# Eight-pass transformer kernel: the first half chunk's maxima turned four steps earlier, and two low parts moved from VectorE to Pool

## Chip, cores and metric

One NeuronCore of a Trainium2 chip runs the kernel. The metric is the device time of one execution in microseconds (us). The time before is 1330.38 us, the median of 3 runs (1329.99 to 1331.14). The profiled execution shown below is another run of the same program.

## The reference

The input x is 2048 tokens by 512 features, in fp32. Four residual layers run one after the other, A, B, A, B, each on the layer norm of x. There are 32 heads of 16 features.

```python
def _A_ref(x, ...):   # linear attention with a learned feature map
    q, k, v = split_heads(x @ wqkv)
    phi_q = concat(softmax(q @ w_phi), softmax(-q @ w_phi))
    phi_k = concat(softmax(k @ w_phi), softmax(-k @ w_phi))
    o = phi_q @ (phi_k.T @ v) / (phi_q @ sum(phi_k) + 1e-6)
    return merge_heads(o) @ wo

def _B_ref(x, ...):   # four segments of 512 tokens, causal softmax plus a memory
    for s in range(4):
        p = softmax(qs @ ks.T * scale + mask)
        o = g * (phi(qs) @ M) / (phi(qs) @ z + 1e-6) + (1 - g) * p @ vs
        M, z = M + phi(ks).T @ vs, z + sum(phi(ks))
    return merge_heads(o) @ wo
```

Only layer B, which runs twice, is touched by the change.

## The kernel before

**Layer B's loop.** Each of the 4 segments has 4 chunks c of 8 heads, and each chunk two half chunks, so that 32 half chunks m are attended in order (m // 8 is the segment). One half chunk takes R = 5 steps of a counter k: `attend` (step m*5 on) makes the five products of keys and queries that become softmax weights. The loop starts at k = BEGIN = -25, so 25 steps run ahead of the first attended product. In them the first queries and keys are projected, while what is left of layer A's second pass (`side`) goes on being computed on the same engines. `steps` writes all of this out; what stands at which step is in tables of text. `BEFORE` is the table for negative k: "k1/2" is two steps of the projection of chunk 1's keys, "v0/2" two steps of a block of values, "max0" the step that is moved here. An entry with "<" ahead is done in front of the step's row work and side work, one without it behind them.

**Row maxima.** Softmax needs each query row's maximum. `maxima(m)` computes the products of a half chunk once more in five rounds, and VectorE (DVE) reduces each to a column of the tile `mxs` by a fused add-mask-and-max with a read of the accumulator behind it. For m = 0 and m = 1 the ten rounds run from k = MAXIMA = -17 to -8, those of m = 0 in the first five. `put_maxima(m)` then turns `mxs` into rows by four 32x32 transposes on DVE into the tile `mt`, and three steps later a DMA on SyncE's queue (SP) writes these rows into row 63 and row 127 of the query tile `e` (tag e8). `attend` multiplies 64 rows where `maxima` multiplied 63; row 63 holds the maxima, so the difference comes out of the matmul. So the first attended product of m, a TensorE (PE) matmul `lg<-e,e`, waits for the transfer `e<-mt`.

**Stacks.** A projection of queries or keys leaves PSUM as `raw` (tag tb3), and `projected` splits it in a high part (ScalarE, tile `ta`) and a low part (raw minus high, line 1075, tile `ta`). `stack(m, side)` copies these three times into the rows of the tile `e` of the chunk's set: three SP DMAs of 128 KB for the queries and three for the keys of a half chunk. `maxima(m)` and `attend(m)` read them. The stack of m = 2, the first of chunk 1, is issued at k = -4 and k = -3; its maxima start at k = 0. The two projections that it needs end at k = -17 (queries) and k = -15 (keys), and their low parts follow a step later. In `projected` all low parts are made by DVE as long as k < R, and by Pool from then on.

**Order.** Every engine's instructions stand in the order in which the program records them (`Ordered` and `held` put each behind the one before it). The fused maxima alone have a higher priority. SP works its queue in order: a DMA that waits for its data holds all behind it. Around the change the SP queue reads: store of a layer A block (`x<-xr`), maxima of m = 0 (`e<-mt`), stack of m = 2 (six times `e<-ta`), stack of m = 3 (six more), maxima of m = 1.

**Names in the trace.** All of the engines' rows but the PE's have line 155 (the helper `Ordered`), matmuls line 177 and PE transposes 181. `g`, `lg`, `mx` and `my` are PSUM tiles (`lg` attended products, `g` also projections and every other round of maxima), `P` the softmax weights or features, `KN` the summed keys of layer A.

Of the kernel before, what the change touches and what calls it, by code (L numbers as in the profile page):

```python
# [7 lines left out]
F32 = mybir.dt.float32  # L8
# [25 lines left out]
R = 5  # L34
# [10 lines left out]
MAXIMA = -17  # L45
# [49 lines left out]
7.0 <max | 7.1 fin P/4              | 7.2 P/5           | 7.3 P/4 | 7.4  # L95
"""
BEFORE = {-25: "load q0", -24: "sq0 sq1", -23: "k0", -22: "sk0 n n", -21: "sk1 v0/2 n n", -20: "v0/2 n n",
          -19: "n n", -18: "v1 n n q1/2", -17: "q1/2", -16: "k1/2", -15: "k1/2", -11: "v2", -9: "max0"}


@with_exitstack
def interleave_kernel(ctx, tc, x_in, a_wqkv, a_wphi, a_wo, b_wq, b_wk, b_wv, b_wo, b_beta,
                      c_ident, c_mask, c_bd, out):
    nc = tc.nc
    MUL, ADD, SUB, MAX, MIN = ALU.mult, ALU.add, ALU.subtract, ALU.max, ALU.min
# [14 lines left out]
    def T2(tag, bufs, dt=F32, shape=(P, 512)):  # L120
        return sp.tile(list(shape), dt, tag=tag, bufs=bufs, name=nm(tag))
# [41 lines left out]
    dve, act, pool, sync = [Ordered(e) for e in (nc.vector, nc.scalar, nc.gpsimd, nc.sync)]  # L163
# [821 lines left out]
    class LayerB:  # L985
# [80 lines left out]
        def projected(self, s, c, m, pp):  # L1066

            d = self.st[s, c]
            hi, lo = d["part", m] = [T2("ta1", TA, F32R) for _ in range(2)]
            raw = T2("tb3", TB3)  # L1070
            act.copy(raw, pp)

            def parts():
                act.copy(hi, raw)
                (pool if self.k >= R else dve).tensor_tensor(out=lo, in0=raw, in1=hi.bitcast(F32), op=SUB)
            todo = [parts]
            if not (s == 0 if m == 0 else s == NSEG - 1):
                e = d["phi", m] = T2("tb2", TB2)

                def features():  # L1080
                    act.activation(e, raw, AF.Relu, scale=-1.0)
                    act.activation(e, e, AF.Exp, scale=-1.0)

                def clipped():
                    act.activation(raw, raw, AF.Relu)

                def added():
                    if m == 0:
                        pool.tensor_scalar(raw, raw, 0.0, None, op0=MAX)
                    pool.tensor_tensor(out=e, in0=raw, in1=e, op=ADD)  # L1090
                todo += [features] + [clipped] * m + [added]
            return todo
# [511 lines left out]
```

## Time and profile before

| What | us |
|---|---|
| median of the runs | 1330.38 (1329.99 to 1331.14) |
| profiled execution, its own time | 1334.12 |
| its span, first to last instruction | 1332.4 |
| PE matmul busy | 1276.0 |
| DVE busy | 1077.4 |
| ACT busy | 834.8 |
| Pool busy | 752.4 |
| mean granted PE clock | 0.99 |

The busy sums are averages over stages with different limits, so the prediction reads one stage: the start of layer B's loop, at 250 to 305 us of the span in the first layer B and at 900 to 955 us in the second. In a row of the timeline stand start, duration, engine, line, operation, tiles and shape, and, in brackets, the time the engine stood idle before it and what ended that.

### The profile page before, as it was taken

How to read it: one execution, taken by the hardware profiler on the slowest of the kernel's cores; microseconds unless marked ns; L12 is line 12 of the kernel's file. 1: busy time of each engine (PE TensorE's matmuls, PEld its weight loads, DVE VectorE, ACT ScalarE, POOL GpSimd, SP SyncE). 2: the span in 40 equal slices, each digit the busy share in tenths (PEclk: the TensorE clock that was granted, in tenths of full speed). 3: DMA queues.
4: the chain of work that ended last, by engine and by line, in shares of the span. 5: the costliest groups of instructions: out<-in, count | busy, mean ns of one | idle time of the engine just before them, and what ended most of it. 6: DMA issues, size and time to landing. Idle time of an engine off the chain costs nothing.

```text
span 1332.4 us, 41983 instructions
## 1 busy us (share of the span) xinstructions
PE 1276.0 (96%) x16488; PEld 989.9 (74%) x16488; DVE 1077.4 (81%) x3503; ACT 834.8 (63%) x1210; POOL 752.4 (56%) x1120
## 2 busy tenths in 40 slices
PE   7999989989999999999999998899899999999987
PEld 6887868857777777777668886787677777777765
DVE  4776678768998998998857766787799999898895
ACT  5556444638778778677644433464477877877754
POOL 1568765405657767666324446562247767776653
PEclk9999999989999999999999998999899999999999
DMA  6388537625555545546451103565446545544432
GB/s 209 104 328 259 168 123 226 185 81 161 166 163 159 168 110 146 164 113 166 136 168 55 64 33 128 171 194 158 111 135 197 172 127 170 147 129 123 121 83 80
DMA packets 134420, 196.59 MB, mean 148 GB/s; under 512 B 15440, under 2 KB 61648, under 8 KB 133456
## 3 DMA queue, kind: packets, MB, share of 16 engines
q1 hardware_dynamic: 133408, 193.80, 48.3%
q8 instruction: 131, 2.15, 0.7%
q14 instruction: 65, 0.53, 0.1%
q10 hardware_dynamic: 816, 0.11, 0.1%
HBM read 101.05 MB, written 39.85 MB: 106 GB/s over the span
## 4 chain that ended last, share of the span: by engine, by line
PE 75%; DVE 16%; ACT 3%; issue 3%; DMA 2%; POOL 1%; SPq 1%; DVEq 0%; ACTq 0%; POOLq 0%
PE g L177 59%; PE lg L177 6%; PE g L181 4%; PE mx L177 3%; DVE g L155 3%; DVE U L155 2%; DVE mx L155 2%; DVE my L155 2%; PE lg L181 2%; PE my L177 1%; DVE es L155 1%; ACT P L155 1%; DVE mxs L155 1%; SPq L155 1%; DMA P<-in 1%
## 5 line engine op out<-in xcount | busy, mean ns | idle before, releaser
L155 ACT ACTIVATE P<-lg 128x1024 f32<-128x1024 f32 x316 | 324.1, 1026 | 98.3 <-PE lg L177 80.1
L155 POOL TENSOR_SCALAR_AFFINE_SELECT P<-P 128x256 f32<-128x256 f32 (+1 forms) x448 | 189.8, 441 | 241.6 <-ACT P L155 223.2
L155 DVE CUSTOM_DVE_ANT_0 mx<-mx,mask 128x512 f32<-128x512 f32 (+2 forms) x316 | 158.9, 503 | 51.2 <-PE my L177 40.7
L155 DVE CUSTOM_DVE_ANT_0 g<-g,mask 128x128 f32<-128x128 f32 (+3 forms) x392 | 189.4, 537 | 6.1 <-PE g L177 5.8
L177 PE MATMUL g<-hh,wqk 64*128 64x512 f32 (+1 forms) x960 | 181.4, 393 | 0.6 <-SPq L155 0.5
L177 PE MATMUL g<-w,oh 64*128 64x512 f32 (+2 forms) x848 | 162.3, 380 | 2.7 <-ACT oh L155 2.6
L155 DVE CUSTOM_DVE_ANT_0 my<-my,mask 128x512 f32<-128x512 f32 (+2 forms) x316 | 163.5, 517 | 0.0
L177 PE MATMUL lg<-e,e 64*128 64x512 f32 (+1 forms) x1010 | 144.8, 343 | 10.5 <-ACT P L155 7.5
L177 PE MATMUL g<-P,v 128*32 128x128 f32 (+3 forms) x2064 | 151.6, 433 | 0.2
L177 PE MATMUL g<-w,hh 64*128 64x512 f32 (+1 forms) x672 | 145.6, 399 | 2.3 <-ACT w L155 1.3
L155 DVE DVE_READ_ACCUMULATOR2_ANT mxs<- 128x1 f32 x1024 | 142.8, 139 | 0.0
L177 PEld LDWEIGHTS lg<-e,e 64*128 64x128 f32 x1010 | 91.5, 184 | 56.3 <-ACT P L155 20.5
L177 PEld LDWEIGHTS g<-hh,wqk 64*128 64x128 f32 (+1 forms) x960 | 97.5, 185 | 20.5 <-SPq L155 2.1
L177 PEld LDWEIGHTS g<-P,v 128*32 128x32 f32 x2064 | 64.9, 109 | 61.2 <-issue 54.4
L177 PEld LDWEIGHTS g<-w,oh 64*128 64x128 f32 (+1 forms) x848 | 95.1, 187 | 19.4 <-ACT oh L155 3.5
L155 ACT COPY tb<-g 128x512 f32<-128x512 f32 (+1 forms) x132 | 71.1, 575 | 51.2 <-PE g L177 51.0
L177 PE MATMUL g<-w,ol 64*128 64x512 f32 (+2 forms) x424 | 102.1, 377 | 1.0 <-DVE ol L155 1.0
L177 PE MATMUL g<-hl,wqk 64*128 64x512 f32 (+1 forms) x480 | 100.2, 389 | 0.0
L177 PEld LDWEIGHTS g<-w,hh 64*128 64x128 f32 (+1 forms) x672 | 84.7, 190 | 19.0 <-ACT w L155 1.6
L177 PE MATMUL mx<-e,e 63*128 63x256 f32 (+3 forms) x323 | 83.1, 320 | 8.4 <-DMA e<-ta 8.3
L177 PE MATMUL g<-w,hl 64*128 64x512 f32 (+1 forms) x336 | 89.9, 395 | 0.0
L155 DVE TENSOR_REDUCE es<-P 128x64 f32<-128x1024 f32 x64 | 77.4, 1209 | 12.9 <-ACT P L155 12.7
(163 smaller groups left out, 2938.2 us busy)
## 6 DMA issues: line engine op xcount, KB each, us to landing
e<-ta SPq DMA_DIRECT2D x384, 128.0 KB
wqk<-wqk SPq DMA_DIRECT2D x128, 256.0 KB
x<-x SPq DMA_DIRECT2D x48, 256.0 KB
pq<-tb SPq DMA_DIRECT2D x24, 256.0 KB
tb<-pq SPq DMA_DIRECT2D x24, 256.0 KB
x<-xr SPq DMA_DIRECT2D x22, 256.0 KB
xr<-x SPq DMA_DIRECT2D x20, 256.0 KB
x<-in SPq DMA_DIRECT2D x16, 256.0 KB
```

What stands on the lines that cost most here:

```text
L155: i = f(*a, **k)
L177: return held(nc.tensor.matmul(*a, **k))
L181: return held(nc.tensor.transpose(*a))
```

## The change

Two edits, both of which act once in each layer B.

```diff
-          -19: "n n", -18: "v1 n n q1/2", -17: "q1/2", -16: "k1/2", -15: "k1/2", -11: "v2", -9: "max0"}
+          -19: "n n", -18: "v1 n n q1/2", -17: "q1/2", -16: "k1/2", -15: "k1/2", -13: "<max0", -11: "v2"}
...
                 act.copy(hi, raw)
-                (pool if self.k >= R else dve).tensor_tensor(out=lo, in0=raw, in1=hi.bitcast(F32), op=SUB)
+                (pool if self.k > MAXIMA else dve).tensor_tensor(out=lo, in0=raw, in1=hi.bitcast(F32), op=SUB)
```

The first moves `put_maxima(0)` from behind the work of step -9 to the front of step -13, right behind the last round of the maxima of m = 0; its DMA is recorded at k = -10 and not at k = -6. The second makes Pool compute low parts from k = -16 on: these are the two of chunk 1. Those of chunk 0 (before k = -17) stay on DVE, and those from k = 5 on were on Pool already.

On DVE, the four transposes `mt<-mxs` stood here, behind four rounds of the maxima of m = 1 and the weighing of layer A's last blocks (`ot<-g,r`) (first layer B; `mxs_2743` holds the maxima of m = 0, `mxs_2744` those of m = 1).

```order
L155 RECIPROCAL r_3626<-g_3617 128x16
L155 TENSOR_TENSOR ot_3571<-g_3617,r_3626 128x256
L155 RECIPROCAL r_3638<-g_3629 128x16
L155 TENSOR_TENSOR ot_3571<-g_3629,r_3638 128x256
L155 STREAM_TRANSPOSE mt_3641<-mxs_2743 32x32 x4
L155 ISA mx_3646,mxs_2744<-mx_3646,mask 128x512
```

In the changed program they stand here on DVE, behind the last maxima of m = 0.

```order
L155 ISA g_3535,mxs_2743<-g_3535,mask 128x512
L155 ISA mxs_2743 128x1
L155 STREAM_TRANSPOSE mt_3542<-mxs_2743 32x32 x4
L155 ISA mx_3550,mxs_2744<-mx_3550,mask 128x128
L155 ISA mxs_2744 128x1
L155 ISA my_3551,mxs_2744<-my_3551,mask 128x128
L155 ISA mxs_2744 128x1
```

Between the two places stand four of the five rounds of maxima of m = 1, the residual add `xr<-g,xr` and two weighings; the transposes are now ahead of all of them. The two low parts leave DVE. On Pool they are added here (same place, first layer B), behind the small operations of a layer norm (`st`).

```order
 L155 TENSOR_TENSOR st_3321<-st_3321 128x4 x2
 L155 TENSOR_SCALAR st_3321<-st_3321 128x4
+L155 TENSOR_TENSOR ta_581_3471<-tb_582_3472,ta_580_3470 128x512
+L155 TENSOR_TENSOR ta_589_3508<-tb_590_3509,ta_588_3507 128x512
 L155 TENSOR_TENSOR P_538_3236<-P_538_3236,rr_3526 128x32x16
 L155 TENSOR_TENSOR tb_591_3511<-tb_590_3509,tb_591_3511 128x512
```

Nothing else on Pool moves. The order of the SP queue, of PE and of ACT stays as it was: the transfer `e<-mt` stands in the same place between the store `x<-xr` and the stack of m = 2. The second layer B is changed in the same way.

## The prediction

> **What bounds the kernel now.** I read the page first, then the waits of PE over the whole span, then the chain of waits around the longest of them, then the timelines of each engine there. On the page PE is busy for nearly the whole span, so time can be won only where PE stands still or runs slowly.
>
> ```profile
> PE 1276.0 (96%) x16488; PEld 989.9 (74%) x16488; DVE 1077.4 (81%) x3503; ACT 834.8 (63%) x1210; POOL 752.4 (56%) x1120
> ```
>
> PE's waits (who waited for what: us in total, times, longest):
>
> ```profile
> PE mx L177 <- DMA e<-ta: 8.3, 2, 4.2
> ...
> PE lg L177 <- DMA e<-mt: 2.9, 3, 1.3
> ```
>
> The first is PE's largest wait, and it occurs just twice, once at the start of each layer B's loop. The chain of waits of the first one (start, us, what), shows who is behind it:
>
> ```profile
> 285.93 0.21 DVE mt L155
> 286.16 0.64 SPq L155
> 286.86 0.56 SPq L155
> ...
> 290.02 2.49 DMA e<-ta
> ...
> 292.65 0.55 PE mx L177
> ```
>
> The last of the four transposes of m = 0's maxima on DVE releases the transfer `e<-mt` on SP's queue. Only then do the stack transfers `e<-ta` behind it start, at 0.6 us each; the sixth starts at 290.02, lands 2.49 us later, and PE's maxima of m = 2 start. So PE waits for the stack of m = 2, and the stack waits on SP behind a transfer that has nothing to do with it. PE's timeline in the first layer B:
>
> ```profile
> 276.68 0.50 PE L177 MATMUL g<-e,e 63*128 63x512 f32 x1 [0.46 <-DVE mxs L155]
> ...
> 277.52 0.71 PE L177 MATMUL g<-w,hh 128*128 128x512 f32 x2
> ...
> 280.44 0.38 PE L177 MATMUL mx<-e,e 63*128 63x256 f32 x1
> ...
> 280.93 0.65 PE L181 MATMUL lg<-ident,P 128*128 128x128 f32 x4
> ...
> 284.50 2.34 PE L177 MATMUL g<-KN,P 128*64 128x68 f32 x64
> 288.09 0.50 PE L177 MATMUL lg<-e,e 64*128 64x512 f32 x2 [1.25 <-DMA e<-mt]
> 292.65 0.55 PE L177 MATMUL mx<-e,e 63*128 63x256 f32 x1 [4.05 <-DMA e<-ta]
> ...
> 298.86 0.51 PE L177 MATMUL lg<-e,e 64*128 64x512 f32 x2
> ```
>
> and in the second:
>
> ```profile
> 927.98 0.50 PE L177 MATMUL g<-e,e 63*128 63x512 f32 x1 [0.46 <-DVE mxs L155]
> ...
> 939.37 0.51 PE L177 MATMUL lg<-e,e 64*128 64x512 f32 x2 [1.23 <-DMA e<-mt]
> 944.11 0.55 PE L177 MATMUL mx<-e,e 63*128 63x256 f32 x1 [4.24 <-DMA e<-ta]
> ...
> 948.95 0.50 PE L177 MATMUL lg<-e,e 64*128 64x512 f32 x2
> ```
>
> Each time three waits: 0.46 us for a bank that DVE still reads, 1.25 (1.23) for the maxima, 4.05 (4.24) for the stack. There is a fourth loss, which no wait shows: behind the gap PE runs at half clock. In the windows (stretch, its length, PE busy, granted clock, DMA share, GB/s):
>
> ```profile
> 288.00:290.00 2.00, 0.50 (x2) 1.00 0.86 196
> ...
> 292.00:294.00 2.00, 1.35 (x5) 0.50 0.84 193
> ...
> 298.00:300.00 2.00, 2.00 (x13) 0.81 0.00 0
> ```
>
> ```profile
> 940.00:942.00 2.00, 0.00 (x0) 0.62 0.89 202
> ...
> 946.00:948.00 2.00, 2.00 (x8) 0.68 0.00 0
> ```
>
> The clock is 0.50 from about 291.9 to 298.8, and from about 940.5 to 947.3.
>
> **The change part by part.** *The transposes.* DVE's timeline:
>
> ```profile
> 269.83 0.69 DVE L155 TENSOR_TENSOR ta<-tb,ta 128x512 fp32r<-128x512 f32 x1 [1.48 <-ACT ta L155]
> ...
> 273.46 0.68 DVE L155 TENSOR_TENSOR ta<-tb,ta 128x512 fp32r<-128x512 f32 x1
> ...
> 277.13 0.33 DVE L155 CUSTOM_DVE_ANT_0 mx<-mx,mask 128x128 f32<-128x128 f32 x1
> ...
> 278.66 0.68 DVE L155 TENSOR_TENSOR xr<-g,xr 128x512 f32<-128x512 f32 x1
> ...
> 285.30 0.83 DVE L155 STREAM_TRANSPOSE mt<-mxs 32x32 f32<-32x32 f32 x4
> 286.17 0.70 DVE L155 CUSTOM_DVE_ANT_0 mx<-mx,mask 128x512 f32<-128x512 f32 x1
> ```
>
> The last maxima of m = 0 are done at 277.13, where those of m = 1 begin; the transposes (0.83 us) come 8.2 us later. They now stand in front of that row. By itself this pushes the residual add `xr` at 278.66 back by 0.83.
>
> *The low parts.* Two DVE rows go, of 0.69 and 0.68 us. At the first DVE had also waited 1.48 us for ACT, while the products of the next round were made. Between 0.7 (one row, the rest taken up by waiting for PE) and 1.4 us (both rows) are won by 277.13; I take 1.4, since DVE's rows run on without a wait from 269.83 to there. The add then starts 0.6 us earlier than before (0.83 - 1.4), at 278.1, with 278.8 as the late end. On Pool they go into a hole:
>
> ```profile
> 265.00 0.23 POOL L155 TENSOR_SCALAR st<-st 128x4 f32<-128x4 f32 x1
> 276.04 1.06 POOL L155 TENSOR_TENSOR P<-P,rr 128x512 f32<-128x512 f32 x1 [10.81 <-DVE rr L155]
> ...
> 310.47 2.54 POOL L155 TENSOR_TENSOR ta<-tb,ta 128x512 fp32r<-128x512 f32 x2
> ```
>
> ```profile
> 271.22 0.62 ACT L155 CAST ta<-tb 128x512 fp32r<-128x512 f32 x1
> ```
>
> Pool takes 1.27 us for one (2.54 for two, third row). The second high part is there at 271.84, so the second low part ends at about 273.1, before 274.1 when DVE ended it. What is queued behind them on Pool, the scaling at 276.04, waits for DVE's `rr` anyhow. Cost: nothing; the cover is a hole of 10.81 us.
>
> *SP's queue.* Its order is unchanged, so the store of the added rows is what now comes last ahead of `e<-mt`:
>
> ```profile
> 279.37 0.33 SPq L155 DMA_DIRECT2D x<-xr  x1
> ...
> 286.86 5.69 SPq L155 DMA_DIRECT2D e<-ta  x9
> ```
>
> The store starts 0.7 us after the add's start, so at 278.8 (late end 279.5). With 0.4 us for it and 0.7 for `e<-mt` (286.16 to 286.86) the first stack transfer starts at 279.9 (280.6) where it was 286.86. The sixth took 292.51 - 286.86 = 5.65 us from there to landing: 285.5 (286.3). The store's own bytes may hold it up. In its window the DMA engines are busy for 0.34 x 2 = 0.7 us:
>
> ```profile
> 280.00:282.00 2.00, 1.00 0.34 128
> ```
>
> so 0 to 0.7 us more, of which I take none, as the transfers overlap.
>
> *When PE needs it.* Without the waits PE goes from the end of `KN` (284.50 + 2.34 = 286.84) into `lg` (0.50), and would reach the maxima of m = 2 at 287.3; with the 0.46 us at 276.68 gone (DVE reads that bank 1.4 us earlier, ahead of the moved transposes), at 286.9. The stack is there 1.4 us before (in the worst case 0.1 us after). The maxima `e<-mt` go out 0.7 us ahead of the stack and are there well before `lg`. So both waits go in full. What is late next is the bank `mx`: DVE reads it at 286.17 plus two rows of 0.7, to 287.4. From the add on, which is 0.6 us earlier (0.1 later at worst), DVE has the same rows as before but for the 0.83 us of the transposes: it is done at 286.0 (286.7), 0.9 us (0.2) before PE asks.
>
> *The half clock.* From the maxima of m = 2 to the next `lg` PE took 298.86 - 292.65 = 6.21 us, and 948.95 - 944.11 = 4.84 in the second. The same work at full clock stands a little earlier: twelve matmuls from 277.52 to 280.44 and the four of the maxima to 280.93, 3.41 us. If there is no gap this loses 2.80 and 1.43 us.
>
> The rule behind this is in the Trainium skill, TensorE: Matmul & The Clock Gate, Part 1: a free-running window of about 3.4 us of idleness halves the clock, a busy one restores it, and its advice is to keep gaps under about 3 us. The trace agrees on the halving and on the length (0.50 for about 6.8 us both times), but is stricter on the gap: in the second layer the clock fell at about 940.5, when PE's second gap was 0.6 us old (939.37 + 0.51 = 939.88), after a gap of 1.23. So a wait of 2 us that stays could cost the clock too.
>
> *Sum.* 1.25 + 1.23 (maxima), 4.05 + 4.24 (stack), 2.80 + 1.43 (clock), 2 x 0.46 (bank) make 15.9 us. Behind this place PE, ACT, DVE and SP go on from one another, so the rest moves as a whole. Against the profiled execution's own 1334.12 this gives 1318.2; it ran 3.74 us above the median of the runs, and I take the gain off the median: 1330.4 - 15.9 = 1314.5. Own bounds: 13.8 won where 0.6 us per layer stays as a wait, most of the store's 0.7, and the bank's 0.46 with it (1316.6); and 17.8 if DVE's 1.4 us pass on to PE whole and not only by 0.46 (2 x 0.94 more: 1312.6).
>
> **The rivals.** (1) *A shorter wait stays.* Pool and DVE may slow one another down. The Trainium skill says, in GPSIMD Engine Reference, Key points, that Pool shares its SBUF interfaces with VectorE and contends with its instructions that have two SBUF inputs. The maxima have one input in PSUM. While Pool makes two low parts at 310.47, DVE's row is
>
> ```profile
> 311.58 0.70 DVE L155 CUSTOM_DVE_ANT_0 mx<-mx,mask 128x512 f32<-128x512 f32 x1 [0.45 <-PE my L177]
> ```
>
> as long as at 286.17 with Pool idle, which speaks against it here. If it did hit, the 2.54 us of Pool's work would cost DVE up to 2.5 us, the stack would land at 288.0, and PE, which keeps its 0.46 and asks at 287.3, would wait 0.7 us per layer: 15.9 - 0.9 - 1.4 = 13.6 won. If such a wait also halves the clock in both layers, 4.2 less: 9.4 won. So 1316.8 to 1321.0; chance 0.15.
>
> (2) *The wait only moves.* The stack's landing is set by something else than SP's order, for instance a DMA rate that sinks, and only the wait for the maxima goes: 1.25 + 1.23, 1327.9. Against it stand the chain, in which SP issues without a pause, and the idle DMA. Chance 0.04.
>
> (3) *No effect,* 1330.4: the early rows of maxima do not free SP, because the store ahead of them, which waits for DVE's add, is as late as the transposes were. The add stands at 278.66, 6.6 us before them; chance 0.03.
>
> (4) *Slower.* The low parts on Pool end last. If Pool comes to them late, the third and fifth stack transfers wait on SP for Pool where they waited for nothing, and everything behind them on SP too. It decides from a low part that ends after 289.4, where the fifth transfer started before (286.86 + 4 x 0.63, as nine took 5.69); each us beyond costs 1 us per layer. Pool's `ta` would have to be 16 us later than the 273.1 above, and Pool has nothing else in its queue; 4 us beyond make 1338. Chance 0.03.
>
> **How the numbers follow.** The forecast has 0.75 and, of its own, 1312.6 to 1316.6. For 8 in 10 the range takes that, the larger part of rival 1 above it, and 1.6 us below it for the spread of the runs (1.15 us) and of the clock's windows: 1311 to 1320. About 0.2% (2.7 us) is what a measurement of this kernel can tell from no change: the forecast, rival 1 and most of rival 2 lie beyond it, 0.93 faster; rival 3 and the rest, 0.04; rival 4, 0.03.
>
> **What would show it.** In the profile after, SP's `e<-ta` of m = 2 start at about 280 (and six to seven us earlier in the second layer too, counted from the same PE matmuls); PE's waits name neither `e<-ta` nor `e<-mt` in these places; the granted clock stays at 1.00 there; from the `KN` rows' end to the second `lg` PE takes about 4 us and not 12. It would be wrong if the wait at `mx` stays over 1 us, if PE's row names Pool or DVE `mxs` instead, or if the clock is still 0.50 there with the wait gone.

## The result, and the profile after

The changed kernel takes 1314.18 us, the median of 4 runs (1313.56 to 1316.51), beside 1330.18 us (1329.49 to 1331.14) of the kernel before: 16.0 us less, ratio 0.9875 with a 95% interval of 0.9860 to 0.9889. The forecast was 1314.5 us, and 15.9 us less. The profiled execution of the changed kernel took 1313.56 us, with a span of 1311.8.

On its page PE, DVE and Pool read

```profile
PE 1269.2 (97%) x16488; PEld 991.8 (76%) x16488; DVE 1075.4 (82%) x3499; ACT 835.4 (64%) x1210; POOL 758.6 (58%) x1124
```

Four instructions went from DVE to Pool (3503 to 3499 and 1120 to 1124), and Pool is busy for 6.2 us longer, though four low parts make 5.2. PE has the same number of matmuls and is busy for 6.8 us less. Most of that is the half clock, in which a matmul takes up to twice as long (1.22 us for the first pair `g<-w,hh` behind the gap in the second layer, where it is 0.71 at full clock): it is gone here, and elsewhere in the span the clock stood at 0.50 for 3.4 us less in this execution. Of PE's waits these are now the longest and the fourth:

```profile
PE lg L177 <- ACT P L155: 7.5, 19, 1.3
...
PE my L177 <- issue: 3.5, 2, 3.1
```

The row `mx <- DMA e<-ta`, the largest before with 8.3 us, is gone, and so is `lg <- DMA e<-mt` with 2.9. PE's timeline at the changed place shows this, in the first layer B and, in the last three rows, in the second:

```profile
263.31 0.56 PE L177 MATMUL g<-e,e 63*128 63x256 f32 x4
...
272.31 0.38 PE L177 MATMUL mx<-e,e 63*128 63x256 f32 x1
272.31 0.38 PE L177 MATMUL my<-e,e 63*128 63x256 f32 x1
...
272.80 0.72 PE L177 MATMUL g<-w,oh 128*128 128x512 f32 x2
...
274.39 0.50 PE L177 MATMUL g<-e,e 63*128 63x512 f32 x2
274.82 0.66 PE L181 MATMUL lg<-ident,P 128*128 128x128 f32 x4
275.23 0.71 PE L177 MATMUL g<-w,hh 128*128 128x512 f32 x2
...
280.76 0.50 PE L177 MATMUL mx<-e,e 63*128 63x512 f32 x1
280.99 0.47 PE L177 MATMUL my<-e,e 63*128 63x512 f32 x1
...
282.41 2.34 PE L177 MATMUL g<-KN,P 128*64 128x68 f32 x64
284.68 0.50 PE L177 MATMUL lg<-e,e 64*128 64x512 f32 x2
285.02 0.28 PE L177 MATMUL mx<-e,e 63*128 63x256 f32 x1
...
288.50 0.49 PE L177 MATMUL lg<-e,e 64*128 64x512 f32 x2
...
924.29 0.50 PE L177 MATMUL lg<-e,e 64*128 64x512 f32 x2
924.63 0.31 PE L177 MATMUL mx<-e,e 63*128 63x256 f32 x1
...
928.14 0.49 PE L177 MATMUL lg<-e,e 64*128 64x512 f32 x2
```

No row has a bracket. From the end of the `KN` rows (282.41 + 2.34) to the second `lg` PE takes 3.75 us where it took 12.0. The queue of SP and the rows of DVE and Pool that feed it:

```profile
278.03 0.33 SPq L155 DMA_DIRECT2D x<-xr  x1
...
279.11 13.68 SPq L155 DMA_DIRECT2D e<-ta  x12
```

```profile
271.71 1.21 DVE L155 TENSOR_REDUCE es<-P 128x64 f32<-128x1024 f32 x1
...
274.95 0.84 DVE L155 STREAM_TRANSPOSE mt<-mxs 32x32 f32<-32x32 f32 x4
...
277.32 0.68 DVE L155 TENSOR_TENSOR xr<-g,xr 128x512 f32<-128x512 f32 x1
...
280.19 0.59 DVE L155 CUSTOM_DVE_ANT_0 my<-my,mask 128x384 f32<-128x384 f32 x1
...
284.09 0.73 DVE L155 CUSTOM_DVE_ANT_0 my<-my,mask 128x512 f32<-128x512 f32 x1
```

```profile
268.88 1.29 POOL L155 TENSOR_TENSOR ta<-tb,ta 128x512 fp32r<-128x512 f32 x1 [4.66 <-ACT ta L155]
271.10 1.30 POOL L155 TENSOR_TENSOR ta<-tb,ta 128x512 fp32r<-128x512 f32 x1 [0.93 <-ACT ta L155]
```

The stack now goes out at 279.11 and not at 286.86, under PE's work. Of the twelve transfers in that row the first six are this stack (the other six are that of m = 3): the sixth goes out at 282.35, 3.24 us behind the first, where it was 3.16. In the windows the DMA share of 0.86 to 0.89, which stood beside an idle PE, now stands beside a busy one:

```profile
282.00:284.00 2.00, 2.00 (x51) 1.69 (x50) 1.93 (x7) 1.01 (x1) 0.00 (x0) 1.00 0.88 199
```

The granted clock is 1.00 (the third column from the right), and DVE, the third engine of the row, is busy for 1.93 of 2.00 us. So DVE is the engine that PE may run into next.

**The gain by piece.** Six rows of PE cut the place in the same way in both programs: the maxima of m = 0 at 263.31, `g<-w,hh` at 275.23, `KN`, the first `lg`, the maxima of m = 2 and the second `lg`. What the prediction's rows of before lack is this:

```profile
264.33 0.56 PE L177 MATMUL g<-e,e 63*128 63x256 f32 x4
...
273.27 0.38 PE L177 MATMUL mx<-e,e 63*128 63x256 f32 x1
273.65 0.38 PE L177 MATMUL my<-e,e 63*128 63x256 f32 x1
...
274.14 0.72 PE L177 MATMUL g<-w,oh 128*128 128x512 f32 x2
...
275.73 0.49 PE L177 MATMUL g<-e,e 63*128 63x512 f32 x1
...
277.11 0.66 PE L181 MATMUL lg<-ident,P 128*128 128x128 f32 x4
...
283.05 0.50 PE L177 MATMUL mx<-e,e 63*128 63x512 f32 x1
```

| Piece, first layer B (second) | before | after | won | the prediction's term |
|---|---|---|---|---|
| maxima of m = 0 to `g<-w,hh` | 13.19 (13.19) | 11.92 (11.91) | 1.27 (1.28) | 0.46 each, bank |
| `g<-w,hh` to `KN` | 6.98 (6.98) | 7.18 (7.17) | -0.20 (-0.19) | none |
| `KN` to the first `lg` | 3.59 (3.57) | 2.27 (2.27) | 1.32 (1.30) | 1.25 (1.23), maxima |
| first `lg` to maxima of m = 2 | 4.56 (4.74) | 0.34 (0.34) | 4.22 (4.40) | 4.05 (4.24), stack |
| maxima of m = 2 to the second `lg` | 6.21 (4.84) | 3.48 (3.51) | 2.73 (1.33) | 2.80 (1.43), clock |
| all | 34.53 (33.32) | 25.19 (25.20) | 9.34 (8.12) | 15.9 in both |

The two places give 17.5 us. The two profiled executions differ by 1334.12 - 1313.56 = 20.6; the other 3.1 lie where the change does nothing. PE's row `my <- issue`, two gaps elsewhere in the span (at 174.9 and 826.0 us), had been longer in the execution before,

```profile
PE my L177 <- issue: 6.0, 2, 4.3
```

and is 2.5 us shorter after. So this pair of executions shows more than the medians, which say 16.0, and part of that is chance.

### The profile page after: what moved, and what is told of

The parts are those of the page before. It is cut to its first block, busy times and chain, and to the rows that moved or that the text cites. A ratio compares the mean times of both kernels' runs of the same rounds, so it can differ in the third digit from the quotient of the medians.

```text
span 1311.8 us, 41989 instructions
## 1 busy us (share of the span) xinstructions
PE 1269.2 (97%) x16488; PEld 991.8 (76%) x16488; DVE 1075.4 (82%) x3499; ACT 835.4 (64%) x1210; POOL 758.6 (58%) x1124
## 3 DMA queue, kind: packets, MB, share of 16 engines
q8 instruction: 131, 2.15, 0.7%
## 4 chain that ended last, share of the span: by engine, by line
PE 79%; DVE 14%; ACT 2%; issue 2%; DMA 2%; POOL 1%; SPq 0%; DVEq 0%; ACTq 0%; POOLq 0%
PE g L177 62%; PE lg L177 6%; PE g L181 4%; PE mx L177 3%; DVE g L155 2%; DVE U L155 2%; PE lg L181 2%; DVE mx L155 2%; DVE my L155 1%; ACT P L155 1%; PE my L177 1%; DVE es L155 1%; POOL P L155 1%; DVE mxs L155 1%; DMA P<-in 1%
## 5 line engine op out<-in xcount | busy, mean ns | idle before, releaser
L177 PE MATMUL g<-hh,wqk 64*128 64x512 f32 (+1 forms) x960 | 185.0, 392 | 0.7 <-SPq L155 0.3
L177 PEld LDWEIGHTS g<-hh,wqk 64*128 64x128 f32 (+1 forms) x960 | 102.7, 185 | 18.1 <-SPq L155 1.6
L177 PE MATMUL g<-hl,wqk 64*128 64x512 f32 (+1 forms) x480 | 103.8, 389 | 0.0
L155 POOL TENSOR_TENSOR ta<-tb,ta 128x512 fp32r<-128x512 f32 x60 | 76.3, 1292 | 14.0 <-ACT ta L155 11.2
```

The lines of the kernel that those rows point to most:

```text
L155: i = f(*a, **k)
L177: return held(nc.tensor.matmul(*a, **k))
```

## The experiments

Theory: PE's waits at the start of layer B's loop come from the order of SP's queue, in which the stack of m = 2 stands behind the maxima of m = 0, and these behind DVE's late transposes; the gap costs clock on top; and the low parts on Pool only make DVE earlier. The rivals: the low parts carry the gain (they, not SP's order, release the stack), the wait only moves, or the half clock has another cause than the gap. The runs came in two groups, each timed beside the kernel before on the same chip (medians 1332.64 and 1333.06 us); the ratios are to that.

### Each edit alone

Only the transposes are moved; the low parts stay on DVE (against the changed kernel):

```diff
-                (pool if self.k > MAXIMA else dve).tensor_tensor(out=lo, in0=raw, in1=hi.bitcast(F32), op=SUB)
+                (pool if self.k >= R else dve).tensor_tensor(out=lo, in0=raw, in1=hi.bitcast(F32), op=SUB)
```

> Only the transposes of m = 0 are moved; the two low parts stay on DVE. Theory (the stack of m = 2 waits on SP's queue behind the transfer of the maxima): the residual add starts at 278.66 + 0.83 = 279.5, the store at 280.2, the first stack transfer at 281.3, the sixth lands at 287.0 to 287.7, and PE asks at 287.3 since the 0.46 us for the bank stays. Both waits and the half clock go: 2.5 + 8.3 + 4.2 = 15.0 us less, 1315.2; up to 0.8 us of wait may stay, 1316. Rival (the gain comes from the relief of DVE by two rows): little is left without them, 2.5 us at most for the maxima, 1327.7.

Measured: 1319.7 us, ratio 0.9902 (0.9886 to 0.9919), 13.0 us of 1330 less. PE's timeline:

```profile
276.53 0.49 PE L177 MATMUL g<-e,e 63*128 63x512 f32 x1 [0.45 <-DVE mxs L155]
...
287.81 0.35 PE L177 MATMUL mx<-e,e 63*128 63x256 f32 x1 [0.42 <-DVE r L155]
...
291.25 0.50 PE L177 MATMUL lg<-e,e 64*128 64x512 f32 x2
```

Both DMA waits and the half clock are gone (287.81 to 291.25 is 3.44 us). So most of the gain is the transposes' alone. On the median of before, 1330.4, that is 1317.3, 1.3 to 2.1 us above what was expected. The wait at the bank stays, as expected. The rows show a part of the difference: since DVE now has the transposes ahead and no relief, it holds `mx` 0.42 us too long, the wait that the prediction named as next late (less in the second layer, where the maxima start 0.51 us behind `lg`; without a wait it is 0.34), and `my` starts 0.30 us behind `mx` (283.20 and 282.90) where both had started together.

The other edit alone, on the kernel before:

```diff
-                (pool if self.k >= R else dve).tensor_tensor(out=lo, in0=raw, in1=hi.bitcast(F32), op=SUB)
+                (pool if self.k > MAXIMA else dve).tensor_tensor(out=lo, in0=raw, in1=hi.bitcast(F32), op=SUB)
```

> Only the two low parts go to Pool; the transposes stay at step -9. Theory: everything on DVE, the transposes too, is 1.3 to 1.4 us earlier, so both waits end that much earlier, but PE also asks 1 us earlier, and the stack still stands behind the maxima: PE's wait for it stays at about 4 us in both layers. 1.3 us won per layer, 1327.6. Rival (relief of DVE): most of the 16 us, 1318 or less.

Measured: 1329.3 us, ratio 0.9979 (0.9965 to 0.9994), 2.8 us less. PE's timeline:

```profile
284.15 0.49 PE L177 MATMUL lg<-e,e 64*128 64x512 f32 x2 [1.26 <-DMA e<-mt]
288.74 0.55 PE L177 MATMUL mx<-e,e 63*128 63x256 f32 x1 [4.10 <-DMA e<-ta]
```

The two waits stand as before, though the low parts are off DVE: the rival that they release the stack falls. The wait at the bank is gone. The two parts, 13.0 and 2.8, make 15.8 against 16.6 for both (0.9875 of 1330): they add up within their intervals.

### SP's order alone

On the kernel before, nothing is computed earlier; the transfer of the maxima of m = 0 is only recorded four steps later, behind the stack of m = 2:

```diff
-            self.at.setdefault(self.k + 3, []).append(
+            self.at.setdefault(self.k + (7 if m == 0 else 3), []).append(
```

> Nothing moves on DVE, Pool, ACT or PE: only SP's transfer of the maxima of m = 0 is recorded behind the stack of m = 2 and not ahead of it. Theory: the stack starts behind the store, at 280.1, and has landed by 286.5; PE's wait for it goes (8.3 us) and the half clock with it (4.2), while the wait for the maxima stays at 1.25 and 1.23 with the bank's 0.46: 12.5 less, 1317.7. If a gap of 1.25 us can halve the clock, up to 4 us less of a gain. Rival (the stack waits for something other than its place on SP, for its data or the DMA engines): no change, 1330.2.

Measured: 1321.42 us, ratio 0.9911 (0.9897 to 0.9926), 11.8 us less. PE, then SP:

```profile
287.32 0.49 PE L177 MATMUL lg<-e,e 64*128 64x512 f32 x2 [1.26 <-DMA e<-mt]
287.66 0.35 PE L177 MATMUL mx<-e,e 63*128 63x256 f32 x1
...
291.10 0.49 PE L177 MATMUL lg<-e,e 64*128 64x512 f32 x2
```

```profile
279.02 4.99 SPq L155 DMA_DIRECT2D e<-ta  x6
285.39 0.63 SPq L155 DMA_DIRECT2D e<-mt  x1
```

This is the run that settles the cause. The transposes are as late as ever and the maxima are waited for as before (1.26), but with the order of two entries of SP's queue exchanged the wait for the stack is gone, and the clock stays up (3.44 us from 287.66 to 291.10). The stack waited for its place in the queue and not for its data: in the kernel before its last low part ended at 274.14 (273.46 + 0.68) and its first transfer went out at 286.86, 12.7 us later.

### The transposes still later

On the kernel before, in its table, `-9: "max0"` becomes

```diff
-          -11: "v2", -9: "max0"}
+          -11: "v2", -8: "max0"}
```

> The kernel before with the transposes of m = 0 one step later (behind one more round of the maxima of m = 1 on DVE, 1.3 us). Theory: SP sends the maxima, and the stack behind them, 1.3 us later; PE's wait for the maxima grows from 1.25 to about 2.5 us in each layer, its wait for the stack stays at 4.1, so 2.6 us more in all: 1.002 of before, in the rows clearer than in the time. Rival (the turn of the maxima is not what the stack waits for): the first wait grows, the second shrinks by as much, no change.

Measured: 1335.08 us, ratio 1.0011 (1.0001 to 1.0022), 1.5 us more where 2.6 were expected, which the interval still holds. PE's timeline:

```profile
290.76 0.49 PE L177 MATMUL lg<-e,e 64*128 64x512 f32 x2 [2.52 <-DMA e<-mt]
295.20 0.55 PE L177 MATMUL mx<-e,e 63*128 63x256 f32 x1 [3.94 <-DMA e<-ta]
```

The first wait grows by 1.27 us, the second doesn't. The second is the time from the landing of the maxima, which starts `lg`, to the landing of the sixth stack transfer, less `lg`'s own 0.50 us; both landings hang on the transposes, and both move with them. So the first wait had no slack at all, and the rival, by which the second would shrink as the first grows, falls. In the second layer the clock was at 0.50 for 10.2 us here.

### The gap filled, to weigh the clock

Two kernels put matmuls of no use into the gaps, on the kernel before (they write into a bank that the next product starts anew). The first adds 14 of 63 rows ahead of the maxima of m = 2:

```diff
+                if m == 2 and what[0] == (0, 0, 0):
+                    k0 = self.sets[0][1]
+                    for _ in range(14):
+                        mm(pb[0], lhsT=k0[0:63, 0, 0:P], rhs=k0[0:63, 0, :],
+                           start=True, stop=True, tile_position=(0, 0))
```

> The kernel before with fourteen matmuls of 512 columns (3.2 us at 0.23 each) on PE in front of the maxima of m = 2, into the bank that these maxima then overwrite, so that PE works in the gap of 4.05 and 4.24 us. Theory (the gap halves the clock): the waits stay as long for the stack, the clock stays at 1.00, and the 2.80 and 1.43 us behind it go: 4.2 less, 1326.0. Rival (these matmuls are slow for another reason, for instance their operands): no change, or slower by what the added matmuls reach beyond the gap, 1330 to 1332.

Measured: 1329.65 us, ratio 0.9979 (0.9966 to 0.9993): neither answer. The clock still fell, but for 3.4 us in each layer. The windows of the second, in which 2.15 us of the gap stayed open (to 940.72):

```profile
941.00:942.00 1.00, 1.00 (x7) 0.68 (x5) 0.72 (x5) 0.00 (x0) 0.00 (x0) 1.00 0.73 168
942.00:943.00 1.00, 1.00 (x5) 0.76 (x3) 0.99 (x6) 0.00 (x0) 0.00 (x0) 0.66 0.00 0
943.00:944.00 1.00, 1.00 (x4) 0.81 (x3) 0.58 (x3) 0.00 (x0) 0.00 (x0) 0.50 0.00 0
```

The clock is cut at about 942.3, when PE has been busy again for 1.6 us. It follows what PE did before. The second kernel fills both gaps, with matmuls of all 128 rows, 5 ahead of the first `lg` and 17 ahead of the maxima of m = 2:

```diff
+                    for _ in range(17):
+                        mm(pb[0], lhsT=k0[:, 0, 0:P], rhs=k0[:, 0, :], start=True, stop=True)
...
+                if m == 0 and kbs == (0,) and r == 0:
+                    k0 = self.sets[0][1]
+                    for _ in range(5):
+                        mm(pb[0], lhsT=k0[:, 0, 0:P], rhs=k0[:, 0, :], start=True, stop=True)
```

> The kernel before, with PE kept at work in both gaps: five matmuls of 512 columns and all 128 rows in front of the first attended product (1.1 us of the 1.25) and seventeen in front of the maxima of m = 2 (3.9 us of 4.05 and 4.24), each into the bank that is overwritten next. The first filling used 63 of 128 rows and left 0.9 and 2.2 us idle, and the clock still fell, for half as long. Theory (the clock follows how busy PE was in the window before): no idle of over 0.4 us is left, the granted clock stays at 1.00 at both places, the stack lands as before, and 2.8 + 1.4 = 4.2 us go: 0.9968 of before. Rival (the slow rows have another cause, or the loss comes back as something else): 0.999 to 1.001.

Measured: 1330.01 us, ratio 0.9978 (0.9964 to 0.9993), 2.9 us less though PE's own work still waits for as long as the transfers take. PE's timeline in the first layer B, then in the second:

```profile
289.50 0.36 PE L177 MATMUL mx<-e,e 63*128 63x256 f32 x1
...
292.93 0.50 PE L177 MATMUL lg<-e,e 64*128 64x512 f32 x2
...
937.34 0.35 PE L177 MATMUL mx<-e,e 63*128 63x256 f32 x1 [0.84 <-DMA e<-ta]
...
940.77 0.49 PE L177 MATMUL lg<-e,e 64*128 64x512 f32 x2
```

From the maxima to the second `lg` it is 3.43 us in both, where it was 6.21 and 4.84: the clock's term is 2.78 + 1.41 = 4.2 us, as predicted, and the gap is its cause. The whole time won only 2.9 (0.9 to 4.8). In the second layer the maxima of m = 2 came 0.7 us later behind `KN` than in the kernel before (1.1 us later in the kernel with 14 matmuls), and SP paused there between two issues of the stack; why is open. That is about half of what lacks to 4.2, and the rest lies within the interval.

### The changed kernel again, and with SP's order exchanged too

In the second group the changed kernel stood once more, unaltered.

> The changed kernel unaltered, beside the others on one chip. Theory: 0.9875 of before as measured, and the low parts on Pool are worth what the bank's wait and the wait for the bank mx cost in the kernel with the moved transposes alone: about 3 us less than that kernel's 0.9902. In its profile no wait for the stack or the maxima in either layer, whatever the clock does elsewhere.

Measured: 1315.74 us, ratio 0.9865 (0.9852 to 0.9879). That is 4.9 us less than the 0.9902 of the transposes alone, where about 3 were expected; the intervals, and the first result's 0.9875, leave room for that. PE's timeline:

```profile
284.82 0.35 PE L177 MATMUL mx<-e,e 63*128 63x256 f32 x1 [0.53 <-DVE r L155]
```

No DMA wait here either, but in this execution PE stands 0.53 us for the bank `mx` where the first profile had none. The place takes 25.96 and 25.48 us, 16.4 less than before; with the first profile's 17.5 that is 16.4 to 17.5, on both sides of the 16.6 that the ratio 0.9875 gives.

The other way round: the changed kernel with the maxima of m = 0 sent behind the stack.

```diff
-            self.at.setdefault(self.k + 3, []).append(
+            self.at.setdefault(self.k + (11 if m == 0 else 3), []).append(
```

> The changed kernel with the transfer of the maxima of m = 0 recorded behind the stack of m = 2 on SP. Theory: with the transposes early neither transfer ends last any more, so the order of the two is worth nothing to the good: the stack lands 0.7 us earlier, unasked; the maxima are issued at about 283 (span time of the profile after) and land at 285, where PE asks at 284.7, so 0 to 1.3 us per layer are lost: ratio to before 0.9875 to 0.9895. Rival (the stack's place on SP still sets the end): faster than the changed kernel by up to 1 us per layer.

Measured: 1317.29 us, ratio 0.9877 (0.9863 to 0.9891), with

```profile
286.83 0.50 PE L177 MATMUL lg<-e,e 64*128 64x512 f32 x2 [0.43 <-DMA e<-mt]
```

and 0.84 us of the same wait in the second layer. The stack is not waited for in either order, and the maxima now come a little late: nothing is left to win in SP's order once the transposes are early. No version measured beats the changed kernel.

## Why the prediction was right, point by point

**The cause.** SP's order was what held the stack, shown by exchanging the two transfers alone (0.9911). Its data was long ready, as the prediction had it from the low parts.

**The waits.** Predicted 2.48 and 8.29, won 2.62 and 8.62. The difference has a plain reason: the idle time of a row counts from the end of the row before it, but without a wait a matmul starts before that end. After the change `lg` starts at 284.68, 0.07 us ahead of the end of `KN` (284.75), and the maxima of m = 2 at 285.02, 0.16 ahead of the end of `lg` (285.18). 1.25 + 0.07 = 1.32 and 4.05 + 0.16 = 4.21, as the table has them.

**The clock.** Predicted 4.23, won 4.06, and 4.2 in the kernel with the gaps filled. The comparison with the same twelve and four matmuls elsewhere (3.41 us) was good to 0.1 us.

**The bank** was the term of the sum that was mis-sized: 0.92 taken, 2.55 won, 2.16 after what came back. The prediction took the 0.46 us that the row showed as idle. In the profile before the two matmuls of that round start 0.95 us apart (275.73, 276.68), and `lg` follows at 277.11, 1.38 us after the first; after, both are one row and `lg` follows 0.43 us after it. So that wait cost 0.95 us, twice what its bracket says, because without it the two run into each other. The other part never had a bracket: at 273.27 and 273.65 `mx` and `my` run one after the other, since DVE reads the banks until then, and from `mx` to `g<-w,oh` it is 0.87 us, after the change 0.49. The two make 1.33 us; smaller shifts both ways, which the rows above don't show, bring the piece to 1.27. The low parts on Pool alone, which left both DMA waits as they were, won 2.8 us, about as much as the bank's 2.55. The prediction's lower end, with DVE's whole 1.4 us passed on, had this case. On the other side stands what it did not name: at 280.99 `my` now starts 0.23 us behind `mx` (at 283.05 before, both together), because DVE, with the transposes ahead of it, reads `my` to 280.78. That gave 0.20 us back in each layer.

**The times of the steps.** The place begins 1.02 us earlier in this execution (263.31 against 264.33). Less that, the add was expected at 277.1 and came at 277.32, the store at 277.8 and 278.03, the first stack transfer at 278.9 and 279.11: each 0.2 late. The prediction had the stack landed 1.4 us before PE asks. Here it was closer: with the 2.49 us that the sixth transfer took to land in the kernel before, it was there at about 284.8 (an estimate: 282.35 + 2.49), 0.2 us before PE's maxima at 285.02. For the next thing late the bank `mx` was named, with 0.9 us to spare. In the first profile of the changed kernel DVE's last row there ends at 284.82, 0.2 us before PE's maxima at 285.02: PE came earlier than reckoned, by the bank's 0.8, and both margins shrank by about as much. In the repeated run that of the bank `mx` was gone (0.53). So, as far as two profiles tell, the forecast hit 15.9 against 16.0 in part by luck, because two small errors met: the bank's larger gain, and the small waits for DVE that come and go.

**The rivals.** That Pool and DVE slow one another down was held off by the trace, and the rows here don't show it either: DVE's sum over `P` at 271.71, beside Pool's low part, took 1.21 us, and with Pool idle before

```profile
274.06 1.21 DVE L155 TENSOR_REDUCE es<-P 128x64 f32<-128x1024 f32 x1
```

also 1.21. The rule that the prediction drew on (the Trainium skill, GPSIMD Engine Reference, Key points) speaks of instructions with two SBUF inputs; DVE had none of those beside the low parts, so it is neither borne out nor refuted by this. That the wait only moves or that nothing happens fell with the trace, and a late Pool with the rows at 268.88 and 271.10: the second low part ends at 272.40, 6.7 us before the first stack transfer.

## What to carry to other kernels

When an engine waits for a transfer, ask first since when its data was ready: if long, look at what stands ahead of it in its queue and what that waits for; exchanging two entries, or making the first one's data earlier, then won nearly the same here (11.8 and 13.0 us). The idle time in a row was a floor for what a wait cost here: where matmuls run into one another the step from start to start, compared with the same pair elsewhere, tells the price, and the gaps on PE cost, in clock behind them, a quarter to a half of their own length again (1.33 us behind 5.5, 2.73 behind 5.3). Once a wait is gone, the engine that is busy all through the place (here DVE, 1.93 of 2.00 us) may take it over, here for tenths of a us.

## What the hardware showed that was not expected

The clock followed a stretch that was past. A window's mean tells when it fell: 0.62 over 940 to 942 is 1.00 for 0.48 us and 0.50 for the rest. It fell at about 940.5 in the second layer of the kernel before, in a gap 0.6 us old behind another of 1.23, and at about 942.3 in the kernel with 14 matmuls of 63 rows, after a gap of 2.15 us, with PE long busy again. In the 3.4 us ahead of these two points PE stood still for 1.23 + 0.6 = 1.83 and for 1.80 us. Where the transposes came still later, it fell at about 293.2 in the first layer (0.60 over 293 to 294), after 2.9 us of idleness, and had not fallen one window sooner, after 1.56; single gaps of 1.26 (SP's order exchanged) and 0.84 us (filled with full rows) were not followed by a fall either. The stretches at 0.50 lasted 3.4, 6.8 and once 10.2 us, whole multiples of one window. The Trainium skill (TensorE: Matmul & The Clock Gate, Part 1) has this window length, which the runs bear out. The advice of the same page (Why this matters for your kernels) of no gap over about 3 us was too generous here, where 1.8 us of idleness in one window were enough.

In the first layer of the kernel with 63 rows the clock fell at about 290.4 (0.69 over 290 to 291), after 3.4 us with only 0.64 us of idleness but 2.8 us of matmuls of 63 rows; full rows kept it at 1.00. That matmuls on half of the rows count for less is one reading; the two kernels also differ in how much of the gaps they fill, and the parts were not tried apart. That stays open.
